# A guarded fallback recurrence moved to another branch, and two gather buffers kept side by side, in a one-core RWKV kernel with two mixtures of experts

## The chip, the cores and the metric

The kernel runs on one core of one Trainium2 chip. The metric is device time in microseconds of one execution. Before the change, three runs took 936.85, 937.87 and 938.58 us; the median is 937.87 us.

## What is computed

Three steps follow each other, each one feeding the next:

```python
# 1. recurrence over S = 768 steps, for B = 4 batches, H = 8 heads, D = 48
cur   = u * k[t] (x) v[t];  y[t] = r[t] . (state + cur)
state = w[t] * state + k[t] (x) v[t]
x = y as rows: N = 3072 tokens, 384 columns
# 2. first mixture, top 1 of E = 8 experts, F = 1024
out[mask] = gate_w * sigmoid(x @ w_output_gate)[e] * (relu(x @ w1[e]) @ w2[e])
# 3. second mixture, top 2 of 8, with noise on the logits
logits += log1p(exp(x @ w_noise)) * noise
out[mask] += top2_w * (relu(x @ w1[e]) @ w2[e])
```

The decays `w` of this input lie between 0.8 and 0.95. The fast form of step 1 is good for decays from 0.625 to 1.25 (`W_MIN`, `W_MAX`); for other decays the kernel holds a step-by-step recurrence that runs only where a flag says so.

## The kernel before, in words

**Step 1** works on 24 blocks of 128 steps (6 chunks times 4 batches), software-pipelined over several stages. Each block's rows go to the DRAM table `xrow`, the block is routed (`Route1`), and for each token an indirect DMA from GpSimd (`scatter`, L106, after a one-element `spacer` memset, L105) writes an entry into `tab1` at the token's place in its expert's list. ScalarE watches the decays (`guard`), and the largest excess becomes `flags[0]` (L373, `flag(wk, 0, ...)`).

**Work laid under step 1.** The first 224 tokens of expert 0 are known before the last blocks are routed. A generator, `early` (L793 to L827), takes them through both layers of expert 0; its steps are spread over the end of step 1 by `take(fill)`, and the rest of them, `take(fill, 99)`, closes it. It is TensorE work: three matmuls for each product (`mm3`, L175 to L177: high times high, low times high, high times low), 128x224 each, with ScalarE (`hh`, L813) and VectorE (`hl`, L814) splitting each hidden block.

**The first branch.** Ahead of that last piece stands `go = nc.values_load(flags[:, 0:1])` and `tc.If(go > 0)` with `recurrence(bank)` inside (L930 to L933). Every engine reads the flag and branches. The flag is 0 here, so the body is jumped over. In the built program the body holds 301 instructions on TensorE, 268 on VectorE, 149 on SyncE, 121 on GpSimd and 90 on ScalarE. After it come the last two scatters into `tab1`, `rank_experts` on VectorE (it sorts the experts by load; L378 to L386), and on SyncE the loads of the entry lists of experts 0, 1 and 2 (`load1`, L485) and of expert 1's weights (`w_load`, L147 and L150, into two `raw` buffers; ScalarE and VectorE split them into high and low parts, L162 and L163).

**First mixture.** For each expert `gather1` (L1097) fetches its rows from `xrow` by indirect DMA, four gathers of up to 118 rows. Expert 0 gathers into buffer `xg10`, expert 1 into `xg11`, expert 2 into `xg10` again. `xg10` stands in the pool `es` from the start. `xg11` is opened at L1086 in the pool `m1`, whose memory belonged to step 1 until then. `xprep1` (L1116 to L1118) turns the rows on TensorE, 3 times 4 transposes for an expert; they stand in steps 5, 6 and 7 of the expert before. `up1` and `down1` are the two layers, the second two steps behind the first. `left_over` (L397) sets `flags[1]` where tokens did not fit into the experts' windows.

**The second branch** (L1261, L1262) stands at the end of the first mixture, with `overflow(0)` inside: the tokens that did not fit. It is not taken either; its body holds 201 instructions on TensorE, 200 on VectorE, 162 on GpSimd, 146 on SyncE, 140 on ScalarE. A third one like it (L1379) ends the second mixture.

**Second mixture.** `gather2` (L1052), `xprep2` (L1069), `up2` and `down2` work the same way, 128 rows at a time. The last short block of an expert multiplies with a float32 copy of w2, which `whole` writes (L1297) into a buffer `w2f` of 2 x 1536 columns.

[...]

Of the kernel before, what the change touches and what calls it, by code (L numbers as in the profile page):

```python
# [9 lines left out]
F32 = mybir.dt.float32  # L10
# [10 lines left out]
N, DM, E, F = B * S, H * D, 8, 1024  # L21
# [23 lines left out]
JE = 2  # L45
# [19 lines left out]
def rwkv_moe_kernel(ctx, tc, r, k, v, w, rT, kT, wT, rkv, u, g1, a1, a2, g2, noise, b1, b2, out):  # L65
# [114 lines left out]
        w_slots(wp, i)  # L180
    es = ctx.enter_context(tc.tile_pool(name="es", bufs=1))
    nz0 = es.tile([128, J1, E], F32, name="nz0")
    xg1 = [es.tile([128, J1, XW], F32, name="xg10")]
    seen = [con.tile([128, 1], F32, name=f"seen{i}") for i in range(2)]


# [209 lines left out]

    def left_over(wk, m, early):  # L397

        n = wk.tile([1, E + 1], F32, name="n")
        w = windows(wk, m)  # L400
        nc.vector.tensor_tensor(n[:, 0:E], base[m][0:1], slot0[0:1], OP.subtract)
        nc.vector.tensor_tensor(n[:, 0:E], n[:, 0:E], w[0:1], OP.subtract)
        nc.vector.tensor_scalar(n[:, E:E + 1], seen[m][0:1], -1.0, float(early), OP.mult, OP.add)
        flag(wk, 1 + m, n, 0.0)


    def recurrence(bank):
        with ExitStack() as c2:
            fb = c2.enter_context(tc.tile_pool(name="fb", bufs=1))
            DQ = D // 4  # L410
            st = fb.tile([128, DQ, D], F32, name="st")
            nc.vector.memset(st, 0.0)
            sel = fb.tile([128, 32], F32, name="sel")
            nc.vector.tensor_copy(sel, ident[:, 0:32])
            for q in range(1, 4):
                nc.vector.tensor_tensor(sel, sel, ident[:, 32 * q:32 * q + 32], OP.add)
            uq = fb.tile([128, DQ], F32, name="uq")
            for q in range(4):
                nc.sync.dma_start(uq[32 * q:32 * q + 32], rows(u, q * DQ, [[0, B], [D, H], [1, DQ]]))

            def over_e(a):
                return a[:, :, None].to_broadcast([128, DQ, D])

            with tc.For_i(0, S // TS, 1) as blk:
                t = {}
                for nm, src in (("r", r), ("k", k), ("w", w), ("v", v)):
                    n = D if nm == "v" else DQ
                    t[nm] = fb.tile([128, TS, n], F32, name="f" + nm)
                    src = src.rearrange("b h s d -> (b h) s d")
                    for q in range(4):  # L430
                        d0 = 0 if nm == "v" else q * DQ
                        nc.sync.dma_start(t[nm][32 * q:32 * q + 32], src[:, bass.ds(blk * TS, TS), d0:d0 + n])
                yq = fb.tile([128, TS, D], F32, name="yq")
                for s in range(TS):
                    kv = fb.tile([128, DQ, D], F32, name="kv")
                    nc.vector.tensor_tensor(kv, over_e(t["k"][:, s, :]),
                                            t["v"][:, s:s + 1, :].to_broadcast([128, DQ, D]), OP.mult)
                    cur = fb.tile([128, DQ, D], F32, name="cur")
                    nc.vector.tensor_tensor(cur, kv, over_e(uq), OP.mult)
                    nc.vector.tensor_tensor(cur, cur, st, OP.add)  # L440
                    nc.vector.tensor_tensor(cur, cur, over_e(t["r"][:, s, :]), OP.mult)
                    nc.vector.tensor_reduce(yq[:, s, :], cur.rearrange("p d e -> p e d"), AX.X, OP.add)
                    nc.vector.tensor_tensor(st, st, over_e(t["w"][:, s, :]), OP.mult)
                    nc.vector.tensor_tensor(st, st, kv, OP.add)
                y = fb.tile([32, TS, D], F32, name="y")
                for h in range(2):
                    p = bank("kp")
                    half = slice(h * TS // 2, (h + 1) * TS // 2)
                    nc.tensor.matmul(p[0:32, 0:TS // 2 * D], sel, yq[:, half, :].rearrange("p a b -> p (a b)"),
                                     start=True, stop=True)  # L450
                    nc.vector.tensor_copy(y[:, half, :].rearrange("p a b -> p (a b)"), p[0:32, 0:TS // 2 * D])
                for b in range(B):
                    dst = xrow[bass.ds(blk * TS + b * S, TS), 0:DM].rearrange("t (h e) -> h t e", h=H)
                    nc.sync.dma_start(dst, y[b * H:(b + 1) * H])
            clear_table(tab1)
            nc.vector.tensor_copy(base[0], slot0)
            nc.vector.memset(seen[0], 0.0)
            nc.vector.memset(ent1[:, 0, 0:JE], 0)
            nc.vector.memset(ent1[:, 0, 0:JE, 0], N)
            for c in range(NC):  # L460
                L = bank("lp")[:, 0:B * 2 * E].rearrange("p (a b) -> p a b", a=B)
                for b in range(B):
                    x = fb.tile([C, DM], F32, name="x")
                    nc.sync.dma_start(x, xrow[b * S + c * C:b * S + (c + 1) * C, 0:DM])
                    p = bank("kp")[:, 0:DM].rearrange("p (a b) -> p a b", a=KD)
                    for j in range(KD):
                        nc.tensor.transpose(p[:, j, :], x[:, j * 128:(j + 1) * 128], ident)
                    xT = fb.tile([128, KD, C], F32, name="xT")
                    nc.scalar.copy(xT, p)
                    for j in range(KD):  # L470
                        nc.tensor.matmul(L[:, b, :], xT[:, j, :], g1s[:, j, :], start=(j == 0), stop=(j == KD - 1))
                g = Route1(fb, L, c * C)
                for _ in g.choose():
                    pass
                g.exps()
                g.rank(bank("kp"))
                for _ in g.place():
                    pass
                for b in range(B):
                    g.enter(b, "tab1 again")  # L480
# [12 lines left out]
    with ExitStack() as c2:  # L493
# [433 lines left out]
        RT[r2].rank(bank("kp"))  # L927
        take(RT[r2].place(), 9)
        take(fill, 2)
        go = nc.values_load(flags[:, 0:1], min_val=0, max_val=1)  # L930
        with tc.If(go > 0):  # L931
            recurrence(bank)
            nc.vector.memset(RT[r2].slot, E * NT)  # L933
        for j in range(RT[r2].nj):
            RT[r2].enter(j, "tab1")
        rank_experts(wk, 0)
# [8 lines left out]


    def overflow(m):
        w1, w2, tab, least, early = ((a1, a2, tab1, min(W1), WE), (b1, b2, tab2, min(W2), NA))[m]
        with ExitStack() as c2:
            fb = c2.enter_context(tc.tile_pool(name=f"ov{m}", bufs=1))  # L950
            bank = banks(psum, p="23", y="5")
# [130 lines left out]
    with ExitStack() as c2:  # L1082
        wk = c2.enter_context(tc.tile_pool(name="m1", bufs=2))
        bank = banks(psum, hp="01", tp="23", yp0="4", yp1="5", yp2="6", lp="7", up="01456")
        X, Q, HT, Y = {}, {}, {}, {}
        xg1.append(wk.tile([128, J1, XW], F32, name="xg11", bufs=1))  # L1086
        GATH, SCAT = [], []

        def part(e):
# [170 lines left out]

    go = nc.values_load(flags[:, 1:2], min_val=0, max_val=1)  # L1261
    with tc.If(go > 0):  # L1262
        overflow(0)


# [4 lines left out]
    with ExitStack() as c2:  # L1270
# [7 lines left out]
            xprep2(POOL[half], e, k, half, bank("tp"))  # L1278


        REST = dict(w=wk.tile([128, 2 * WH], F32, name="w2f"), h=wk.tile([128, NF, 64], F32, name="hf"))

        def quarters(q):
            return 4 if q <= 32 else 2 if q <= 64 else 1
# [151 lines left out]
```

## Time and profile before

| | us |
|---|---|
| median of three runs | 937.87 |
| the profiled execution | 937.88 |
| its span, first to last instruction | 936.2 |
| TensorE busy | 892.2 (95%) |
| VectorE busy | 516.2 (55%) |
| GpSimd busy | 402.7 (43%) |
| ScalarE busy | 395.3 (42%) |
| mean granted TensorE clock | 0.974 |

In the rows of this document PE is TensorE's matmul, PEld its weight load, DVE VectorE, ACT ScalarE, POOL GpSimd and SP SyncE; a name with q (PEldq, SPq) is that engine's instruction queue. `out<-in` are the program's names of the tiles. What stands in brackets at the end of a row is how long the engine was idle before it and what ended that. Tile `b` is a bank of PSUM, `xg` a gathered block of rows, `ent` an entry list, `tab` a table of entries.

### The profile page before, as it was taken

The numbers are of one execution on the slowest core, as the hardware profiler recorded it, in microseconds if no ns is written. First come the engines' busy times: TensorE is split into PE (matmuls) and PEld (weight loads), VectorE is DVE, ScalarE is ACT, GpSimd is POOL, SyncE is SP. The second block draws the span as 40 slices with busy tenths as digits, with TensorE's granted clock in tenths as the row PEclk, the third lists the DMA queues.
The fourth block names the chain that finished last, engine by engine and source line by source line (L and its number), as shares of the span: only waits on it lengthen the run. The fifth ranks groups of instructions, "written<-read, shape, count | busy, mean of one in ns | idle before, by whom it ended". The sixth has DMA issues, their size and how long they took to land. (4 is left out here: it accounts for less than half of the span.)

```text
span 936.2 us, 16625 instructions
## 1 busy us (share of the span) xinstructions
PE 892.2 (95%) x6244; PEld 797.3 (85%) x6244; DVE 516.2 (55%) x1146; ACT 395.3 (42%) x862; POOL 402.7 (43%) x562
## 2 busy tenths in 40 slices
PE   8999999979799999999898999999999999999996
PEld 4887777769788999999787989889898998989995
DVE  7999999754355565556561555272543627244220
ACT  4556555333345455555441443342433425344320
POOL 3234554334244885598564441423424133242212
PEclk9999998799899999999998999999999999999998
DMA  9777664014645767676514653435444444443203
GB/s 206 180 212 181 180 172 140 28 37 132 182 124 136 183 166 174 151 185 131 160 26 106 148 134 85 76 115 104 104 88 92 133 76 122 102 102 85 34 9 44
DMA packets 91099, 113.39 MB, mean 121 GB/s; under 512 B 26002, under 2 KB 68895, under 8 KB 91000
## 3 DMA queue, kind: packets, MB, share of 16 engines
q1 hardware_dynamic: 65848, 80.87, 30.9%
q0 software_dynamic: 25152, 31.27, 18.3%
q8 instruction: 53, 0.87, 0.4%
q14 instruction: 46, 0.38, 0.2%
HBM read 86.96 MB, written 25.78 MB: 120 GB/s over the span
## 5 line engine op out<-in xcount | busy, mean ns | idle before, releaser
L106 POOL DMA_INDIRECT out<-yo,ent x54 | 84.6, 1567 | 275.6 <-ACT yo L1327 232.8
L175 PE MATMUL b<-xhi,w1h 128*128 128x512 f32 (+8 forms) x384 | 133.0, 346 | 0.0
L177 PE MATMUL b<-xhi,w1l 128*128 128x512 f32 (+8 forms) x384 | 132.1, 344 | 0.0
L176 PE MATMUL b<-xlo,w1h 128*128 128x512 f32 (+8 forms) x384 | 132.1, 344 | 0.0
L1071 DVE TENSOR_TENSOR xlo<-b,xhi 128x512 fp32r<-128x512 f32 (+8 forms) x48 | 27.1, 570 | 155.4 <-ACT xhi L1070 142.4
L1327 ACT ACTIVATE yo<-b,ent 128x384 f32<-128x384 f32 (+1 forms) x48 | 27.9, 582 | 166.8 <-issue 128.1
L1314 PE MATMUL b<-w2h,hah 128*128 128x384 f32 x256 | 88.8, 347 | 0.4 <-PEq L1262 0.4
L106 POOL DMA_INDIRECT tab<-en,si x60 | 79.8, 1330 | 19.0 <-issue 13.9
L1316 PE MATMUL b<-w2h,hal 128*128 128x384 f32 x256 | 86.9, 339 | 0.0
L1315 PE MATMUL b<-w2l,hah 128*128 128x384 f32 x256 | 86.8, 339 | 0.0
L175 PEld LDWEIGHTS b<-xhi,w1h 128*128 128x128 f32 x384 | 72.3, 188 | 11.8 <-issue 3.1
L647 POOL TENSOR_SCALAR_AFFINE_SELECT at<-at 128x512 f32<-128x512 f32 x48 | 38.8, 833 | 98.3 <-ACT at L646 98.3
L175 PE MATMUL b<-xh,w1h 128*128 128x224 f32 (+7 forms) x216 | 76.3, 353 | 3.8 <-PEq L931 3.1
L176 PEld LDWEIGHTS b<-xlo,w1h 128*128 128x128 f32 x384 | 72.4, 188 | 8.8 <-DVE xlo L1071 0.2
L177 PEld LDWEIGHTS b<-xhi,w1l 128*128 128x128 f32 x384 | 72.3, 188 | 8.6
L175 PE MATMUL b<-hh,w2h 128*128 128x224 f32 (+7 forms) x216 | 74.7, 346 | 0.0
L176 PE MATMUL b<-xl,w1h 128*128 128x224 f32 (+7 forms) x216 | 73.5, 340 | 0.1
L177 PE MATMUL b<-xh,w1l 128*128 128x224 f32 (+7 forms) x216 | 73.4, 340 | 0.0
L163 DVE TENSOR_TENSOR w1l<-raw,w1h 128x512 fp32r<-128x512 f32 x92 | 61.7, 685 | 21.0 <-ACT w1h L162 20.4
L1080 DVE SCALAR_TENSOR_TENSOR hal<-b,hah 128x512 fp32r<-128x512 f32 x64 | 44.2, 691 | 52.4 <-ACT hah L1079 52.2
L176 PE MATMUL b<-hl,w2h 128*128 128x224 f32 (+7 forms) x216 | 72.7, 336 | 0.0
L177 PE MATMUL b<-hh,w2l 128*128 128x224 f32 (+7 forms) x216 | 72.5, 336 | 0.0
(221 smaller groups left out, 2153.7 us busy)
## 6 DMA issues: line engine op xcount, KB each, us to landing
raw<-in_a SPq DMA_DIRECT2D x32, 768.0 KB, 9.5
raw<-in_b SPq DMA_DIRECT2D x30, 768.0 KB, 4.5
decay<-in_wT SPq DMA_DIRECT2D x24, 224.0 KB, 3.4
kT<-in_kT SPq DMA_DIRECT2D x24, 224.0 KB, 5.9
rT<-in_rT SPq DMA_DIRECT2D x24, 224.0 KB, 4.3
v<-in_rkv SPq DMA_DIRECT2D x24, 192.0 KB, 4.4
xrow<-x SPq DMA_DIRECT2D x24, 192.0 KB, 3.3
out<-z SPq DMA_DIRECT2D x6, 768.0 KB
```

The lines of the kernel that those rows point to most:

```text
L106: st = nc.gpsimd.indirect_dma_start(out=table, out_offset=bass.IndirectOffsetOnAxis(ap=idx, axis=0), in_=src, in_offset=None, bounds_check ...
L163: eng.tensor_tensor(c, a, b.bitcast(F32), OP.subtract)
L175: nc.tensor.matmul(ps, st[0], mv[0], start=start, stop=False)
L176: nc.tensor.matmul(ps, st[0], mv[1], start=False, stop=False)
L177: nc.tensor.matmul(ps, st[1], mv[0], start=False, stop=stop)
L647: nc.gpsimd.affine_select(at[:, hh], at[:, hh], [[0, HP], [1, C]], OP.is_gt, 0.0, base=0, channel_multiplier=-1)
L1071: nc.vector.tensor_tensor(t["lo"][:, k], p[:, 0:n], t["hi"][:, k].bitcast(F32), OP.subtract)
L1080: nc.vector.scalar_tensor_tensor(l, p[:, 0:n], 0.0, h.bitcast(F32), OP.max, OP.subtract)
L1314: nc.tensor.matmul(parts[0], h[:, f, sl], wh, start=(f == 0), stop=False)
L1315: nc.tensor.matmul(parts[0], h[:, f, sl], wl, start=False, stop=False)
L1316: nc.tensor.matmul(parts[0], l[:, f, sl], wh, start=False, stop=(f == NF - 1))
L1327: nc.scalar.activation(o, y, AF.Copy, scale=wgt2[:q, e, j:j + 1])
```

## The change

The recurrence goes from the first branch into the second, under a branch of its own; `left_over` puts `flags[0]` beside the other counts, so that the second branch is taken where either flag is set. What the first mixture then wrote from wrong rows is cleared and done again in `overflow(0)`, which starts at slot 0 (`least` is 0). Both gather buffers of the first mixture become halves of one tile `xgs` in `es`, open from the start to the end of the kernel; the float32 copy of w2 lies in that tile.

```diff
@@ pools
-    xg1 = [es.tile([128, J1, XW], F32, name="xg10")]
+    xgs = es.tile([128, 2 * J1 * XW], F32, name="xg1")
+    xg1 = [xgs[:, i * J1 * XW:(i + 1) * J1 * XW].rearrange("p (a b) -> p a b", a=J1) for i in range(2)]
@@ left_over
-        n = wk.tile([1, E + 1], F32, name="n")
+        n = wk.tile([1, E + 2], F32, name="n")
+        if m == 0:
+            nc.vector.tensor_copy(n[:, E + 1:E + 2], flags[:, 0:1])
+        else:
+            nc.vector.memset(n[:, E + 1:E + 2], 0.0)
@@ recurrence (its end)
             clear_table(tab1)
-            nc.vector.tensor_copy(base[0], slot0)
-            nc.vector.memset(seen[0], 0.0)
-            nc.vector.memset(ent1[:, 0, 0:JE], 0)
-            nc.vector.memset(ent1[:, 0, 0:JE, 0], N)
+            clear_table(tab2)
+            for t in base:
+                nc.vector.tensor_copy(t, slot0)
+            nc.vector.memset(seen[0], float(WE))
...
@@ the end of step 1
         take(fill, 2)
-        go = nc.values_load(flags[:, 0:1], min_val=0, max_val=1)
-        with tc.If(go > 0):
-            recurrence(bank)
-            nc.vector.memset(RT[r2].slot, E * NT)
         for j in range(RT[r2].nj):
             RT[r2].enter(j, "tab1")
@@ overflow
-        w1, w2, tab, least, early = ((a1, a2, tab1, min(W1), WE), (b1, b2, tab2, min(W2), NA))[m]
+        w1, w2, tab, least, early = ((a1, a2, tab1, 0, WE), (b1, b2, tab2, min(W2), NA))[m]
@@ first mixture
-        xg1.append(wk.tile([128, J1, XW], F32, name="xg11", bufs=1))
@@ the second branch
     go = nc.values_load(flags[:, 1:2], min_val=0, max_val=1)
     with tc.If(go > 0):
+        again = nc.values_load(flags[:, 0:1], min_val=0, max_val=1)
+        with tc.If(again > 0):
+            recurrence(banks(psum, kp="2", lp="7"))
         overflow(0)
@@ second mixture
-        REST = dict(w=wk.tile([128, 2 * WH], F32, name="w2f"), h=wk.tile([128, NF, 64], F32, name="hf"))
+        REST = dict(w=xgs[:, 0:2 * WH], h=wk.tile([128, NF, 64], F32, name="hf"))
```

In the built program of the change the second branch's body holds 515 instructions on TensorE, 488 on VectorE, 318 on SyncE, 301 on GpSimd and 242 on ScalarE. Outside the bodies each engine keeps the order of its work: the reads of the first flag and the first branch go, VectorE gets one instruction more in each `left_over`, and what wrote and read `w2f` names `xg`.

**GpSimd from the first branch to expert 1's gathers.** Before, from the end of the jump (semaphores in brackets are waited for; DMASW are those of GpSimd's DMAs, DMAHW those of SyncE's; `xg_107` is xg10, `xg_4008` is xg11; the 112-row gathers are expert 0's, the 118-row ones expert 1's):

```order
L931 ISA [waits Pool_49,DMASW4_49,DMASW5_49,DMASW3_49,DMASW6_49,DMASW2_49,DMASW7_49,DMASW1_49,DMASW0_49]
L931 UNCONDITIONAL_BRANCH
L105 MEMSET spacer 1x1 [waits Pool_49]
L106 DMA tab_66<-ent,slot 25600x2 [waits DMASW7_49,DMAHW7_49,DMASW0_49,DVE_49]
L105 MEMSET spacer 1x1 [waits Pool_49]
L106 DMA tab_66<-ent,slot 25600x2 [waits DMASW1_49]
L1097 DMA xg_107<-xrow,ent_81 112x392 [waits DMAHW4_49,DMAHW5_49,DMAHW3_49,DMAHW6_49,DMAHW0_49,DMASW2_49]
L1097 DMA xg_107<-xrow,ent_81 112x392 [waits DMASW3_49]
L1097 DMA xg_4008<-xrow,ent_81 118x392 [waits DMAHW2_49,DMAHW1_49,DMAHW3_49,DMASW6_49,DMAHW4_49,DMASW5_49,DMAHW5_49,DMASW4_49,DMAHW6_49,DVE_49,DMAHW7_49,PE_49,Activation_49]
L1097 DMA xg_4008<-xrow,ent_81 118x392 x3
```

And now (L1102 is the line of the gathers, L1119 that of the copy of the noise columns):

```order
L300 IOTA ent 128x2 [waits DMASW5_49,DMASW4_49]
L105 MEMSET spacer 1x1 [waits Pool_49]
L106 DMA tab_66<-ent,slot 25600x2 [waits DVE_49,Pool_49]
L105 MEMSET spacer 1x1 [waits Pool_49]
L106 DMA tab_66<-ent,slot 25600x2
L1102 DMA xg_107<-xrow,ent_81 112x392 [waits DMAHW6_49,DMAHW5_49,DMAHW7_49,DMAHW4_49,DMAHW3_49]
L1102 DMA xg_107<-xrow,ent_81 112x392
L1102 DMA xg_107<-xrow,ent_81 118x392 [waits DMAHW0_49]
L1102 DMA xg_107<-xrow,ent_81 118x392
L1102 DMA xg_107<-xrow,ent_81 118x392 [waits DMASW6_49]
L1102 DMA xg_107<-xrow,ent_81 118x392 [waits DMASW7_49]
L1119 COPY nz_106<-xg_107 112x16 [waits DMASW3_49,DMASW2_49]
```

The jump with its waits on all of GpSimd's own DMAs is gone, and expert 1's first gather waits for its entry list alone, not for VectorE, TensorE and ScalarE to be done with the memory of step 1.

**TensorE at the first branch.** Before (the rows of L424 stand in the body that is jumped over):

```order
L175 MATMUL b_2924<-hh,w2h_97 128x224
L176 MATMUL b_2924<-hl,w2h_97 128x224
L177 MATMUL b_2924<-hh,w2l_98 128x224
L930 TENSOR_LOAD flags [waits DVE_49]
L931 COMPARE_AND_BRANCH
L424 COMPARE_AND_BRANCH
```

And now:

```order
L175 MATMUL b_2924<-hh,w2h_97 128x224
L176 MATMUL b_2924<-hl,w2h_97 128x224
L177 MATMUL b_2924<-hh,w2l_98 128x224
L175 MATMUL b_2980<-xh,w1h_95 128x224 [waits DVE_49]
L176 MATMUL b_2980<-xl,w1h_95 128x224
L177 MATMUL b_2980<-xh,w1l_96 128x224
```

The matmuls of the next step of `early` follow directly.

**TensorE at the second branch.** Now (L429 is the first line of the recurrence that branches; before, the reading of the flag and one branch, L1261 and L1262, stood in the same place):

```order
L175 MATMUL b_6509<-xhi_6124,w1h_3126 128x512
L176 MATMUL b_6509<-xlo_6125,w1h_3126 128x512
L177 MATMUL b_6509<-xhi_6124,w1l_3127 128x512
L1266 TENSOR_LOAD flags [waits DVE_49]
L1267 COMPARE_AND_BRANCH
L1268 TENSOR_LOAD flags
L1269 COMPARE_AND_BRANCH
L429 COMPARE_AND_BRANCH
```

The second pair, L1268 and L1269, stands inside the first body and is jumped over with it.

## Rows read from the trace of the kernel before

**Rows 1.** The profile's page, busy time of each engine.

```profile
PE 892.2 (95%) x6244; PEld 797.3 (85%) x6244; DVE 516.2 (55%) x1146; ACT 395.3 (42%) x862; POOL 402.7 (43%) x562
```

**Rows 2.** Stretches: width, busy PE, PEld, DVE, ACT, POOL (count), granted clock, DMA share, GB/s.

```profile
200.00:222.00 22.00, 18.25 (x148) 17.79 (x146) 7.31 (x36) 3.92 (x14) 6.33 (x10) 0.92 0.31 93
222.00:250.00 28.00, 21.68 (x148) 20.55 (x149) 14.20 (x32) 11.79 (x28) 12.70 (x12) 0.82 0.55 134
...
400.00:450.00 50.00, 50.00 (x312) 47.65 (x311) 30.48 (x83) 25.83 (x56) 43.82 (x55) 1.00 0.63 146
```

**Rows 3.** One line's instructions, L931, the first branch: queue, count, ns, starts.

```profile
L931 POOLq EVENT_SEMAPHORE  x5: 17/43/43, 203.3 to 206.9; - x5
...
L931 PEldq COMPARE_BRANCH  x1: 4501/4501/4501, 203.0 to 203.0; - x1
```

**Rows 4.** TensorE in order of time, around the first branch: start, us.

```profile
207.71 0.40 PE L175 MATMUL b<-xh,w1h 128*128 128x224 f32 x1 [3.14 <-PEq L931]
...
211.30 0.28 PE L177 MATMUL b<-hh,w2l 128*128 128x224 f32 x1
...
212.42 0.27 PE L175 MATMUL b<-hh,w2h 128*128 128x224 f32 x1
```

**Rows 5.** GpSimd in order of time, from the first branch to expert 1's gathers.

```profile
207.75 0.09 POOL L105 MEMSET spacer<- 1x1 f32 x1 [4.44 <-DMA tab<-ent,slot]
...
215.55 0.97 POOL L1097 DMA_INDIRECT xg<-xrow,ent  x1 [4.31 <-issue]
...
223.93 1.65 POOL L1097 DMA_INDIRECT xg<-xrow,ent  x1 [6.17 <-ACT xh L1117]
...
229.79 2.15 POOL L1097 DMA_INDIRECT xg<-xrow,ent  x1 [0.30 <-issue]
```

**Rows 6.** TensorE in order of time, expert 1's first transposes and what follows.

```profile
234.66 0.26 PE L1116 MATMUL b<-ident,xg 118*128 118x118 f32 x1
235.11 0.32 PE L1116 MATMUL b<-ident,xg 118*128 118x118 f32 x1 [0.18 <-DMA xg<-xrow,ent]
239.76 0.46 PE L1116 MATMUL b<-ident,xg 118*128 118x118 f32 x1 [4.33 <-DMA xg<-xrow,ent]
241.19 0.46 PE L1116 MATMUL b<-ident,xg 118*128 118x118 f32 x1 [0.97 <-DMA xg<-xrow,ent]
241.32 0.54 PE L175 MATMUL b<-hh,w2h 128*128 128x224 f32 x1
...
245.28 0.63 PE L1116 MATMUL b<-ident,xg 118*128 118x118 f32 x4
```

**Rows 7.** Stretches 208 to 211 and 222 to 228, columns as in group 2.

```profile
208.00:211.00 3.00, 3.00 (x16) 3.00 (x16) 1.78 (x8) 0.36 (x1) 1.83 (x3) 0.50 0.04 9
...
222.00:228.00 6.00, 5.16 (x29) 4.77 (x30) 3.85 (x13) 3.27 (x10) 3.46 (x3) 0.74 0.06 8
```

**Rows 8.** Expert 1's weights: SyncE's issue and ScalarE's first split in order of time.

```profile
228.82 0.39 SPq L147 DMA_DIRECT2D raw<-in_a  x1
```

**Rows 9.** ScalarE in order of time, the first split of that load.

```profile
238.31 0.62 ACT L162 CAST w1h<-raw 128x512 fp32r<-128x512 f32 x1 [5.10 <-DMA raw<-in_a]
```

**Rows 10.** Tile raw from 190 to 300 us, its loads.

```profile
DMA to landing us min/median/max: 7.3/8.4/9.5
```

**Rows 11.** One line's instructions, L1262, the second branch.

```profile
L1262 PEldq EVENT_SEMAPHORE  x2: 51/51/51, 493.6 to 493.8; - x2
...
L1262 PEldq COMPARE_BRANCH  x1: 362/362/362, 489.7 to 489.7; - x1
...
L1262 DVEq COMPARE_BRANCH  x1: 63/63/63, 494.7 to 494.7; - x1
```

**Rows 12.** TensorE's first wait for gathered rows after the second branch.

```profile
504.39 0.75 PE L1069 MATMUL b<-ident,xg 128*128 128x128 f32 x2 [1.72 <-DMA xg<-xrow,ent]
```

**Rows 13.** GpSimd's first gather after the second branch, in order of time.

```profile
500.11 1.00 POOL L1052 DMA_INDIRECT xg<-xrow,ent  x1 [5.52 <-DMA ent<-tab]
```

**Rows 14.** VectorE in order of time, one element in left_over.

```profile
222.42 0.13 DVE L403 TENSOR_SCALAR n<-seen 1x1 f32<-1x1 f32 x1
```

More of the change, by code (lines that the diff above doesn't have):

```diff
@@ L404, in left_over, with recurrence @@
         flag(wk, 1 + m, n, 0.0)
-    def recurrence(bank):
+    def recurrence(bank, r=r, k=k, v=v, w=w, u=u):
         with ExitStack() as c2:
@@ L455, in recurrence @@
             clear_table(tab1)
-            nc.vector.tensor_copy(base[0], slot0)
-            nc.vector.memset(seen[0], 0.0)
-            nc.vector.memset(ent1[:, 0, 0:JE], 0)
-            nc.vector.memset(ent1[:, 0, 0:JE, 0], N)
+            clear_table(tab2)
+            for t in base:
+                nc.vector.tensor_copy(t, slot0)
+            nc.vector.memset(seen[0], float(WE))
+            nc.vector.memset(seen[1], 0.0)
+            nc.vector.memset(place_of[0], 0.0)
+            nc.vector.memset(ent2[:, 0, 0:CUT], 0)
+            nc.vector.memset(ent2[:, 0, 0:CUT, 0], N)
             for c in range(NC):
```

## The prediction, made before the change was run

> **What bounds the kernel now.** I read the page first: TensorE is busy for 892.2 of 936.2 us, no other engine for more than 516.2 [rows 1]. So the time can only fall where TensorE stands still or runs slowly. The view by stretches says where. In the stretch from 400 to 450 us, in the first mixture, TensorE has work all the time at full clock. Between 200 and 250 us it has not: it is busy for 18.25 of 22 us and then for 21.68 of 28, at a granted clock of 0.92 and 0.82 [rows 2]. In these 50 us stand both things that the change touches, so I read TensorE, GpSimd and the queues there in order of time.
>
> Two holes are to be seen. At the first branch TensorE's queue spends 4.501 us in the jump [rows 3], and the array waits 3.14 us, from 204.57 to 207.71 [rows 4]. GpSimd waits 4.44 us there, for its own scatters to land [rows 5]. The second hole is at expert 1's first transposes. TensorE waits 0.18, 4.33 and 0.97 us for gathered rows [rows 6], because GpSimd began expert 1's gathers only at 223.93, 6.17 us after it was free [rows 5]. The name beside that wait, ScalarE's `xh`, is only what came last; by the order in the section on the change the gather waited for three engines to leave step 1's memory, where `xg11` was opened.
>
> After each hole comes a slow stretch. [...] After the second hole eighteen matmuls take from 241.32 to 245.28, 0.220 each [rows 6].
>
> **The change, part by part.**
>
> *The first branch goes.* TensorE gets back the wait of 3.14 us. It then had no hole, and I take it that the slow stretch behind it goes too: 3.59 us for seventeen steps against 17 x 0.112 = 1.90, so 1.69. Bounds for this term: 0 and 1.69; I take 1.69, since the same matmuls ran at 0.112 just behind. Together 4.83. The chain beside it gains as much: GpSimd's last two scatters no longer stand behind 207.75, where its wait of 4.44 us ended [rows 5]. Entry lists, expert 0's gathers (from 215.55 [rows 5]) and expert 1's first weight loads follow these scatters; with 4.4 to 4.8 us they stay where they were against TensorE. `rank_experts`, seven short VectorE instructions, now runs between two steps of `early`; TensorE's second layer runs two steps behind the first and covers it.
>
> *Expert 1's gathers wait for their list alone.* They follow expert 0's two, of 0.97 us and 0.3 of issue each: 215.55 - 4.8 + 2 x 1.27 = 213.3. From the first to the fourth it was 5.86 us, and the fourth took 2.15 [rows 5], so GpSimd starts the fourth near 219.2. TensorE comes to these transposes at 234.66 - 4.83 = 229.8 [rows 6]. The fourth gather landed by 241.19, 11.4 us after its start at 229.79, beside two weight loads. As slow as that again, it would land at 219.2 + 11.4 = 230.6 and cost 0.8; if it lands in 10.6 or less it costs nothing. So 0.18 + 4.33 + 0.97 = 5.48 us go, and with them the slow stretch: 3.96 - 18 x 0.112 = 1.94. Bounds here: 6.6 and 7.4. I take 7.42, for the loads that it runs beside start 4 us and more before the gathers and not, as then, in their midst.
>
> *What is late next.* Expert 1's second half of w1 is loaded into a buffer that its first half must leave, so its issue at 228.82 [rows 8] moves with TensorE, to 224.0, and no further. Before, ScalarE got it at 238.31 after a wait of 5.10 [rows 9], 9.5 us after the issue; that was hidden behind the wait for the gathers. Without them TensorE would go through the last three steps of expert 0 in some 6.5 us from 229.8. ScalarE stands at that load with the next hidden block behind it. At 9.5 us the data come at 233.5, and TensorE waits about 1.3 us for that block and 0.7 for the last transposed columns behind the fourth load. At 7.3 us, the shortest of these loads [rows 10], it waits for nothing. I take 1.0, for the median of 8.4, between 0 and 2.0.
>
> *The second branch jumps further.* TensorE jumped 301 instructions in 4.501 us [rows 3] and 201 in 0.362 [rows 11]; now it is 515 there, so I take the long price. Its queue reached this branch at 489.7, but its array had work until 493.6 [rows 11]. A jump until 494.2 makes it 0.6 late, and that falls into its wait of 1.72 for the next gather [rows 12]. That gather, GpSimd's at 500.11 [rows 13], waits for its list and for every engine to have passed the branch. VectorE is the last to come, at 494.7 [rows 11]; with 4.5 us it is through at 499.2, so 0.9 us are left. Cost: 0. Bounds: 0 and, if nothing hid it, 4.501 - 0.362 = 4.1. [...]
>
> *Edits at no cost.* One element more in each `left_over` is one VectorE instruction of about 0.13 us [rows 14], on an engine that then waits for ScalarE. `xgs` instead of `w2f`: the same instructions on the same data, long after the last gather into it. The recurrence's and the overflow's new lines are not run.
>
> *Sum.* 3.14 + 1.69 + 5.48 + 1.94 - 1.0 = 11.25 us. The profiled execution took 937.88 us, 0.01 above the median of the three runs, so the forecast is 937.88 - 11.25 = **926.6 us**. I let it reach the end because TensorE is full in the first mixture behind expert 1's start, as in the stretch from 400, and GpSimd's part there, though it is busy for 43.82 of 50 us [rows 2], starts from what TensorE gives it.
>
> **The rivals.**
>
> *The transfers take the wait's place.* Expert 1's gathers now run beside its first two weight loads, and expert 2's beside the next two. If they hold each other up as the load of 9.5 us was held up [rows 9], TensorE stands at the same place as before and only the branch is won: 937.88 - 4.83 = 933.0. For it speaks that ScalarE waited for that load until 238.31, just ahead of 239.76 [rows 6]; against it that expert 1's gathers start 10.6 us earlier, 213.3 and not 223.93, and so share the transfers' engines with other loads over a longer stretch.
>
> *The second branch takes it back.* Place: L1267, on the engine that leaves it last, which GpSimd's gather at 500.11 [rows 13] waits for. Price: each microsecond that the longest jump takes over 5.4 (500.11 - 494.7) is one microsecond at the end. Twice 4.501 would give 926.6 + 3.6 = 930.2. It decides when the jump lasts over 5.4 + 11.25 = 16.7 us: then the kernel is slower than 937.9. Nothing in the trace jumps for longer than 4.501.
>
> *The gain is lost on the way.* If GpSimd's chain of scatters, not TensorE, sets when the second mixture can start, arriving 11 us early at it means waiting 11 us longer: 937.9. Its 43.82 of 50 us [rows 2] speak for it; against it, that TensorE does not wait at all in that stretch.
>
> **How the numbers follow.** Forecast 0.80, range of its own 924 to 928.5. Transfers 0.10 (933.0). Second branch, part given back, 0.04 (930.2), all of it and more 0.03 (over 939.8 if the jump lasts over 18.6 us). Lost on the way 0.03 (937.9). The range for all takes in: no new wait, 925.6; in addition the slow stretch that I left in, between 222 and 228 us, where the clock was 0.74 [rows 7], that is 3.1 us at half speed, worth 1.6 if it goes: 924.0; a microsecond for the spread of runs (936.85 to 938.58): 923.0. Upwards the transfers' case and half a microsecond, 933.5. A measurement of this kernel can tell 0.2%, 1.9 us, from no change: faster 0.80 + 0.10 + 0.04 = 0.94, the same 0.03, slower 0.03.
>
> **What would show it.** Right: no matmul idle near 204.6 and none at half clock until 211; the 118-row gathers' first start near 213; no wait of L1121 (the transposes' new line) for `xg` over 1 us; TensorE's transposes of expert 1 from about 229.8 on; a long jump at L1267 on TensorE and VectorE with GpSimd's next gather not later against the last scatter than before. Wrong in size: a wait of ScalarE for `raw` that ends after 234 and a TensorE hole behind it. Wrong altogether: the second mixture starting at the same time as before, or a jump at L1267 that ends after GpSimd's list has landed.

## The result, and the profile after

The changed kernel took 925.76 us, the median of four runs (924.22 to 928.43), against 938.23 for the kernel before in the same runs: a ratio of 0.9871, 95% interval 0.9837 to 0.9905. The profiled execution spans 925.3 us and the one before 936.2, so 10.9 us have to be found.

The page, and the stretches of [rows 1, 2], of the changed kernel:

```profile
PE 889.2 (96%) x6244; PEld 795.3 (86%) x6244; DVE 515.4 (56%) x1148; ACT 395.5 (43%) x862; POOL 402.6 (44%) x562
```

```profile
200.00:222.00 22.00, 19.90 (x155) 19.11 (x154) 7.83 (x38) 4.79 (x16) 12.22 (x15) 0.89 0.39 110
222.00:250.00 28.00, 28.00 (x201) 25.75 (x201) 16.00 (x29) 15.53 (x35) 5.17 (x7) 0.98 0.67 203
...
198.00:204.00 6.00, 6.00 (x42) 5.93 (x43) 4.17 (x28) 1.45 (x6) 2.34 (x6) 0.72 0.03 3
...
220.00:224.00 4.00, 4.00 (x24) 4.00 (x24) 1.75 (x4) 1.99 (x5) 0.72 (x2) 0.61 0.35 93
```

From 222 to 250 TensorE is busy for all 28 us, where it was for 21.68. Two slow stretches are left, 198 to 204 (clock 0.72) and 220 to 224 (0.61).

TensorE in order of time, the places of [rows 4, 6] and then the second branch and the gathers behind it:

```profile
205.91 0.27 PE L177 MATMUL b<-hh,w2l 128*128 128x224 f32 x1
...
217.22 0.29 PE L1121 MATMUL b<-ident,xg 112*128 112x112 f32 x1 [0.99 <-DMA xg<-xrow,ent]
218.39 0.70 PE L1121 MATMUL b<-ident,xg 112*128 112x112 f32 x5 [0.88 <-DMA xg<-xrow,ent]
...
230.34 0.57 PE L1121 MATMUL b<-ident,xg 118*128 118x118 f32 x4
...
232.76 0.57 PE L1121 MATMUL b<-ident,xg 118*128 118x118 f32 x4
...
485.94 0.65 PE L1322 MATMUL b<-w2h,hah 128*128 128x384 f32 x1 [4.55 <-DVEq L1267]
...
497.39 0.27 PE L1075 MATMUL b<-ident,xg 58*128 58x58 f32 x1 [0.99 <-DMA xg<-xrow,ent]
```

The matmul that began at 211.30 [rows 4] now begins at 205.91, 5.39 earlier: the hole at the first branch is gone. The transposes of 245.28 [rows 6] now begin at 232.76, 12.52 earlier: the wait for expert 1's rows is gone too. New are two waits for expert 0's rows (0.99, 0.88) and a hole of 4.55 us behind the second branch. Matmuls are matched in this way below: by order, one trace against the other; what the lead grows over a stretch is what that stretch gained.

GpSimd, the places of [rows 5, 13]:

```profile
210.51 0.96 POOL L1102 DMA_INDIRECT xg<-xrow,ent  x1 [4.35 <-DMA ent<-tab]
...
213.03 1.65 POOL L1102 DMA_INDIRECT xg<-xrow,ent  x1 [0.30 <-issue]
...
218.87 1.64 POOL L1102 DMA_INDIRECT xg<-xrow,ent  x1 [0.30 <-issue]
...
481.09 1.30 POOL L106 DMA_INDIRECT tab<-en,si  x1 [0.22 <-issue]
...
490.48 1.00 POOL L1058 DMA_INDIRECT xg<-xrow,ent  x1 [8.08 <-DMA ent<-tab]
```

Expert 1's gathers follow expert 0's at once, and not 6.17 us later [rows 5].

ScalarE's split of the load of [rows 9], and the second branch's line, as in [rows 11]:

```profile
230.29 0.62 ACT L162 CAST w1h<-raw 128x512 fp32r<-128x512 f32 x1 [1.40 <-DMA raw<-in_a]
```

```profile
L1267 POOLq EVENT_SEMAPHORE  x6: 17/30/1521, 483.4 to 485.4; - x6
...
L1267 DVEq EVENT_SEMAPHORE  x2: 21/21/21, 485.8 to 485.9; - x2
...
L1267 PEldq COMPARE_BRANCH  x1: 3657/3657/3657, 477.6 to 477.6; - x1
...
L1267 DVEq COMPARE_BRANCH  x1: 72/72/72, 482.7 to 482.7; - x1
```

TensorE's queue has its 3.66 us while the array still has work, until 481.4. VectorE comes to the branch at 482.7 and is through 3.1 us later, and TensorE's next matmul waits until then.

### The profile page after: what moved, and what is told of

The parts are those of the page before. It is cut to its first block, busy times and chain, and to the rows that moved or that the text cites. A ratio compares the mean times of both kernels' runs of the same rounds, so it can differ in the third digit from the quotient of the medians.

```text
span 925.3 us, 16594 instructions
## 1 busy us (share of the span) xinstructions
PE 889.2 (96%) x6244; PEld 795.3 (86%) x6244; DVE 515.4 (56%) x1148; ACT 395.5 (43%) x862; POOL 402.6 (44%) x562
## 4 chain that ended last, share of the span: by engine, by line
PE 71%; DVE 8%; DMA 7%; issue 7%; POOL 3%; ACT 3%; SPq 0%; POOLq 0%; DVEq 0%; ACTq 0%
PE b L175 14%; PE b L176 13%; PE b L177 13%; PE b L1322 6%; PE b L1324 6%; PE b L1323 6%; PE b L1075 2%; PE b L719 2%; DMA xg<-xrow,ent 2%; DVE cp L634 1%; DMA tab<-en,si 1%; PE b L652 1%; PE b L1318 1%; POOL out L106 1%; DVE g L622 1%
## 6 DMA issues: line engine op xcount, KB each, us to landing
decay<-in_wT SPq DMA_DIRECT2D x24, 224.0 KB, 3.9
kT<-in_kT SPq DMA_DIRECT2D x24, 224.0 KB, 4.7
rT<-in_rT SPq DMA_DIRECT2D x24, 224.0 KB, 5.9
```

## The experiments

Where the 10.9 us lie is read from this table: for each kernel, what a stretch gained against the trace of the kernel before (us; the stretches are in that trace's time; negative is lost).

| stretch | after | again (e10) | again (e8) | e1 | e2 | e3 | e4 | e5 | e6 | e7 | e9 | e11 | e12 |
|---|---|---|---|---|---|---|---|---|---|---|---|---|---|
| 199.9 to 213.5, first branch | 3.84 | 3.84 | 3.84 | 0.28 | 3.82 | 3.31 | 4.61 | 3.83 | 3.27 | 4.98 | 3.83 | 3.83 | 3.83 |
| 213.5 to 232, expert 0's rows | -1.08 | -1.18 | 1.48 | -0.47 | -0.73 | -0.07 | -1.54 | -1.30 | -2.95 | 1.49 | -1.17 | -1.35 | -0.89 |
| 232 to 248, expert 1's rows | 8.26 | 8.25 | 8.15 | 8.26 | 0.70 | 8.25 | 0.99 | 8.25 | 8.25 | 3.86 | 8.24 | 8.25 | 8.25 |
| 476 to 515, second branch | -0.50 | 0.56 | -0.13 | -1.06 | 0.68 | 0.07 | 0.47 | -1.88 | 2.81 | 0.19 | 2.69 | -1.33 | 0.14 |

For the changed kernel the rest is 1.55 up to 199.9, -0.40 from 248 to 476 and -0.72 from 515 on; no edit touches the first and the last of these. Where e1 to e8, e11 and e12 ran, the kernel before itself took longer (952.69 us beside e1 to e4, 949.05 beside e5 to e8, 960.99 beside e11 and e12; 938.82 beside e9 and e10), and the traces there have further holes between 248 and 476 that the first two traces, e9 and e10 don't have; so these kernels are read by stretch, and by ratio only roughly.

**Each half of the change alone.** e1 is the kernel before with

```diff
-    xg1 = [es.tile([128, J1, XW], F32, name="xg10")]
+    xgs = es.tile([128, 2 * J1 * XW], F32, name="xg1")
+    xg1 = [xgs[...] for i in range(2)]
-        xg1.append(wk.tile([128, J1, XW], F32, name="xg11", bufs=1))
-        REST = dict(w=wk.tile([128, 2 * WH], F32, name="w2f"), ...)
+        REST = dict(w=xgs[:, 0:2 * WH], ...)
```

> The kernel before with both gather buffers standing through and w2's float32 copy in them; the first branch keeps the recurrence. Two causes (my theory): the wait of TensorE for expert 1's rows goes (5.48 us and the slow stretch behind it, 1.94), the hole of 3.1 us at the first branch stays: 937.9 - 7.4 = 930.5 us, up to 931.5 if ScalarE's wait for expert 1's second load costs 1. Rival A, the branch alone was worth it and the transfers keep expert 1's rows late: 936 to 938, with the wait at expert 1's first transposes still over 3 us.

e2 is the changed kernel with these lines back as they were.

> The changed kernel with the second gather buffer and the float32 copy back where they were; only the recurrence is moved. My theory: no hole near 204, the wait at expert 1's first transposes stays, 5 us earlier: 937.9 - 4.8 = 933.1 us, and 1 less gained if the longer second jump costs something. Rival A: 926. Rival B, the longer jump takes back what the shorter first gave: 936 to 938. If the two parts add up, the gains of this kernel and of the one with the buffers alone sum to the 11 to 12 us of the change.

Measured: e1 0.9936 of the time before (0.9891 to 0.9981), e2 0.9962 (0.9924 to 1.0001). In order of time, e1 and then e2, TensorE and GpSimd:

```profile
206.62 0.34 PE L175 MATMUL b<-xh,w1h 128*128 128x224 f32 x1 [2.86 <-PEq L932]
...
234.03 0.57 PE L1116 MATMUL b<-ident,xg 118*128 118x118 f32 x4
```

```profile
232.52 0.32 PE L1121 MATMUL b<-ident,xg 118*128 118x118 f32 x1 [2.74 <-DMA xg<-xrow,ent]
...
235.04 0.46 PE L1121 MATMUL b<-ident,xg 118*128 118x118 f32 x1 [2.20 <-DMA xg<-xrow,ent]
```

```profile
218.01 1.65 POOL L1102 DMA_INDIRECT xg<-xrow,ent  x1 [6.22 <-PE b L1121]
```

With the buffers alone the hole at the branch stays and the wait for expert 1's rows goes; with the branch alone it is the other way round, and GpSimd again waits some 6 us for engines to leave step 1's memory. Over the first three stretches e1 gains 8.07 and e2 3.79; together 11.86, the change 11.02. The two causes add up, so rival A falls: each half gains at its own place and nothing at the other's. Rival B falls too, since e2's last stretch lost nothing.

**The longer second jump.** e3 leaves the recurrence for other decays out:

```diff
-        again = nc.values_load(flags[:, 0:1], min_val=0, max_val=1)
-        with tc.If(again > 0):
-            recurrence(banks(psum, kp="2", lp="7"))
         overflow(0)
```

> The changed kernel without the recurrence for other decays at all (its way for such inputs is left out; the rest is unchanged), so the second branch jumps 201 instructions on TensorE and 200 on VectorE as before. Theory C: the hole of 4.55 us at L1322 behind the second branch is VectorE's jump, and it goes, but the list of gathered rows is late next, so 0.5 to 1.5 us are gained: 924.3 to 925.3 us. Rival D: the hole and the slow stretch behind it stand on the path and all of 4.55 + 1.7 comes back: 919.5. Rival E, which I forecast: 0, 925.8.

Measured: 0.9837 (0.9795 to 0.9879); the interval would hold theory D too, so the stretch decides. TensorE in order of time, and the branch's line:

```profile
498.21 0.41 PE L1319 MATMUL b<-w2h,hah 128*128 128x384 f32 x1 [0.52 <-PEq L1267]
507.78 0.59 PE L1075 MATMUL b<-ident,xg 128*128 128x128 f32 x2 [0.88 <-DMA xg<-xrow,ent]
510.58 0.36 PE L1075 MATMUL b<-ident,xg 58*128 58x58 f32 x1 [2.21 <-DMA xg<-xrow,ent]
```

```profile
L1267 DVEq EVENT_SEMAPHORE  x2: 21/21/21, 499.6 to 499.7; - x2
...
L1267 PEldq COMPARE_BRANCH  x1: 3654/3654/3654, 493.9 to 493.9; - x1
...
L1267 DVEq COMPARE_BRANCH  x1: 72/72/72, 499.0 to 499.0; - x1
```

VectorE passes in 0.6 us and the hole is 0.52, but TensorE then waits 0.88 and 2.21 for gathered rows. The stretch gives 0.07, amid the 0.56, -0.13 and -0.50 of the kernel with the recurrence in it: rival D falls. Theory C is right about the hole, which is VectorE's passage; of its gain nothing is to be seen, as rival E forecasts, though among executions that differ by 1.06 us a gain of 0.5 would not be seen either. TensorE's own queue took its 3.65 us here too, so the hole of 4.55 was not its own jump.

**The length of the first jump.** e4 is the kernel before with the recurrence's loop over chunks cut to a quarter:

```diff
-            for c in range(NC):
+            for c in range(NC // 4):
```

> The kernel before with the recurrence under its first branch cut to a quarter of its chunks (its way for other decays is left incomplete; TensorE has 76 instructions to jump and not 301, VectorE 173 and not 268). My theory, the hole is the jump's length and GpSimd's wait is a second matter: TensorE has no hole at the first branch and its jump takes under 0.5 us; GpSimd still waits some 4.4 us there, so expert 0's gathers stay near 215.5 and TensorE waits 3 to 5 us for them; expert 1's gathers come 4 to 5 us earlier and TensorE waits under 1.5 us for those: 932 to 934 us. Rival F, the hole is the flag's reading or GpSimd's wait and not the jump: the hole stays at 3 us, 937.9.

Measured: 0.9941 (0.9905 to 0.9976). The first branch's line, then the second branch's (L1262), and TensorE in order of time:

```profile
L931 POOLq EVENT_SEMAPHORE  x3: 17/17/43, 202.3 to 202.5; - x3
...
L931 PEldq COMPARE_BRANCH  x1: 358/358/358, 202.0 to 202.0; - x1
...
L1262 PEldq COMPARE_BRANCH  x1: 3530/3530/3530, 496.5 to 496.5; - x1
...
L1262 DVEq EVENT_SEMAPHORE  x2: 21/21/21, 504.7 to 504.8; - x2
```

```profile
218.21 1.12 PE L1116 MATMUL b<-ident,xg 112*128 112x112 f32 x6 [2.19 <-DMA xg<-xrow,ent]
...
232.26 0.32 PE L1116 MATMUL b<-ident,xg 118*128 118x118 f32 x1 [1.30 <-DMA xg<-xrow,ent]
235.60 0.46 PE L1116 MATMUL b<-ident,xg 118*128 118x118 f32 x1 [3.01 <-DMA xg<-xrow,ent]
```

The jump took 0.358 us instead of 4.501 [rows 3] and the hole is gone: it was the body that is jumped over, not the flag's reading, so rival F falls. The time is the one expected (0.9941 of 937.9 is 932.4), but by another sum: TensorE waits 2.19 us for expert 0's rows and not 3 to 5, and 4.31 for expert 1's and not under 1.5. GpSimd did not wait 4.4 us: it was through its semaphores at 202.5, not 206.9 [rows 3], so its wait too belonged to the body. Expert 1's gathers kept their wait, as in e2.

e4 shows one thing more. It leaves the second branch as it was, 201 instructions on TensorE and 200 on VectorE, and only shortens the code ahead of it; yet TensorE's queue takes 3.530 us there and not 0.362 [rows 11], and VectorE, which comes at 501.5, 3.2 us and not 0.6. So the number of instructions jumped over does not set the price.

**The hole behind the second branch.** e5 puts two of the eight blocks of `ahead` behind the branch:

```diff
-        for f in range(3, NF):
+        for f in range(3, 6):
             ahead(f)
...
         overflow(0)
+    for f in range(6, NF):
+        ahead(f)
```

> The changed kernel with the last two of the eight hidden blocks that are computed ahead (18 matmuls of 0.233 us) put behind the second branch instead of ahead of it, so that TensorE has 4.2 us of work while VectorE jumps. Theory G: the hole of 4.55 us at L1322 goes, but the chain from GpSimd's last scatter to the gathered rows is as long as before and is late next; TensorE waits 3 to 5 us more for xg behind it and the time stays within 1 us of the changed kernel's. Rival D: the hole stood on the path, 4 to 6 us are gained.

Measured: 0.9910 (0.9875 to 0.9946), beside 0.9899 for the changed kernel in the same runs. TensorE in order of time:

```profile
495.60 0.47 PE L175 MATMUL b<-xhi,w1h 128*128 128x512 f32 x1 [0.41 <-PEq L1267]
511.59 0.47 PE L1075 MATMUL b<-ident,xg 128*128 128x128 f32 x2 [3.12 <-DMA xg<-xrow,ent]
514.55 0.35 PE L1075 MATMUL b<-ident,xg 58*128 58x58 f32 x1 [2.49 <-DMA xg<-xrow,ent]
```

Theory G in kind: the hole is 0.41 and the waits for rows are 5.61 together; rival D falls again. In size it was worse than expected, 1.4 to 2.4 us less in the stretch than the three executions of the changed kernel.

e6 has, besides, the last expert's slots earlier:

```diff
         for k in range(KD):
+            if k == 1 and between:
+                between()
...
-        ahead(2)
-        routing_b(e)
+        ahead(2, lambda: routing_b(e))
+        route2_c(Q[e], T1[e][0], "tab2")
         rank_experts(wk, 1)
         w_split(1, 0, W2B, 2)
-        route2_c(Q[e], T1[e][0], "tab2")
```

> As the kernel with two blocks behind the branch, and the last expert's ranks and slots (routing_b) are computed in the middle of the third block ahead, not behind it, with rank_experts and one split of weights behind the scatters' issue, so GpSimd's six last scatters start 1.5 to 2 us earlier against TensorE. Theory G: the chain of scatters, list and gathers sets the end here, so 1.5 to 2.5 us are gained on the changed kernel. Rival: if TensorE's work or VectorE's jump sets it, nothing is gained.

Measured: 0.9885 (0.9824 to 0.9946), and 2.81 in the stretch, in a profiled execution that was the longest of the four (947.75 us; the others 933.16 to 945.05). So the reading rests on e9, the same kernel again in more executions, beside the changed kernel.

> The kernel with the ranks and slots earlier and two blocks behind the branch, again with more rounds: by the stretch from the second branch on it gained some 3 us on the changed kernel, so a ratio to the kernel before that is 0.003 lower than the changed kernel's in these same runs. Rival: its gain there was chance like the waits at L1121, and the two ratios agree.

> The changed kernel beside it: 0.985 to 0.990 of the time before, hole of 4.5 us at L1322, a gain of 3.8 us at the first branch and of 9 us at expert 1's rows against the trace of the kernel before.

Measured: 922.96 us for e9, 0.9824 (0.9794 to 0.9854); 924.60 for e10, 0.9842 (0.9815 to 0.9869). In e9, GpSimd's first of the six scatters and TensorE:

```profile
475.79 1.30 POOL L106 DMA_INDIRECT tab<-en,si  x1 [1.31 <-DVE s L360]
```

```profile
483.14 0.47 PE L175 MATMUL b<-xhi,w1h 128*128 128x512 f32 x1 [1.40 <-DVE hal L1088]
498.74 0.27 PE L1075 MATMUL b<-ident,xg 58*128 58x58 f32 x1 [2.48 <-DMA xg<-xrow,ent]
```

GpSimd's wait for VectorE there is 1.31 instead of 3.09 us, and the stretch gains 2.69, 2.13 more than in e10. It comes twice, in e6 and e9. The times are 0.0018 apart and not the 0.003 expected; their intervals overlap, so e9 beats the kernel before for certain and the changed kernel by its trace only.

**Which wait the hole was.** Why should TensorE, with hidden blocks to multiply, wait for VectorE to pass? Its first matmul behind the branch writes PSUM bank 7, and the recurrence, now in the body, has its logits there. e11 moves them:

```diff
-            recurrence(banks(psum, kp="2", lp="7"))
+            recurrence(banks(psum, kp="2", lp="3"))
```

> The changed kernel with the recurrence's logits in PSUM bank 3 instead of bank 7, and nothing else. Theory K: TensorE's hole of 4.55 us behind the second branch is no jump of its own and no data that it needs; its first matmul there writes bank 7, which VectorE reads inside the body that is jumped over, so it waits until VectorE has passed the branch. With bank 3 the hole falls to 0.5 us. The list of gathered rows is late next, so TensorE waits 3 to 4 us for xg instead of 1 and the stretch from 476 to 515 changes by less than 1 us: 0.984 to 0.988 of the time before. Rival: VectorE's last hidden block is what the matmul waits for; then the hole stays at 4.5.

e12 adds the earlier slots of e6, with all eight blocks ahead of the branch.

> Bank 3 as beside it, and the last expert's ranks and slots in the middle of the third block ahead as in the kernel that did best, but all eight blocks ahead of the branch as in the changed kernel. If the list sets the end of this place and the hole is only bank 7, the stretch gains 2 to 3 us on the changed kernel as with two blocks behind the branch: 0.981 to 0.985 of the time before. Rival: the two blocks behind the branch were what gained; then the stretch stays within 1 us of the changed kernel's.

Measured: e11 0.9893 (0.9834 to 0.9951), e12 0.9862 (0.9801 to 0.9923). The branch's line and TensorE of e11:

```profile
L1267 PEldq COMPARE_BRANCH  x1: 3417/3417/3417, 503.5 to 503.5; - x1
...
L1267 DVEq COMPARE_BRANCH  x1: 72/72/72, 508.5 to 508.5; - x1
```

```profile
507.68 0.42 PE L1322 MATMUL b<-w2h,hah 128*128 128x384 f32 x1 [0.45 <-PEq L1267]
...
519.50 0.82 PE L1075 MATMUL b<-ident,xg 128*128 128x128 f32 x2 [3.00 <-DMA xg<-xrow,ent]
522.26 0.35 PE L1075 MATMUL b<-ident,xg 58*128 58x58 f32 x1 [1.94 <-DMA xg<-xrow,ent]
```

Theory K: with another bank TensorE goes on at 507.68, before VectorE has even come to the branch (508.5), and the hole is 0.45. e4 shows the same from the other side: its second body has no recurrence in it and does not name bank 7, VectorE is through only at 504.8, and TensorE goes on at 500.86 after 0.45 us. In e11 the waits for rows take the hole's place, 4.94 us, and the stretch ends at -1.33; the hole was hidden time to a microsecond. e12's stretch is 0.14: there its rival stands, the earlier slots alone gain nothing. In e12 SyncE issued the list at 504.75 and the gather began 4.59 us later, where e9 has 3.11 (488.30 to 491.41). The profile names a matmul as what the gather waited for; the queue's own rows tell more, GpSimd's at the gather's line and VectorE's behind the branch:

```profile
L1058 POOLq EVENT_SEMAPHORE  x12: 17/43/2802, 504.8 to 508.5; - x12
```

```profile
L1268 DVEq EVENT_SEMAPHORE  x2: 21/21/21, 507.8 to 507.9; - x2
```

The wait of 2.80 us ends at 507.98, 0.04 after VectorE's last signal behind the branch, and it is that signal's semaphore that it waits for. So the gather needs its list and VectorE's passage. In e12 the list is early and VectorE late, since all its hidden blocks come ahead of the branch; in e9, with two of them behind it, VectorE is through at 486.8, ahead of the list's issue; in e5 VectorE is through at 499.7 and the list is issued only at 504.57. So e5, e11 and e12 gain nothing, and e6 and e9, with the slots earlier and the blocks behind, gain 2.7 to 2.8: it takes both.

**Expert 0's rows.** e7 issues expert 1's first two weight loads on GpSimd's queue behind expert 0's gathers; e8 is the changed kernel again.

```diff
-        w_load(0, 1, W1A)
-        w_load(0, 1, W2A)
...
         gather1(0)
+        for w in (W1A, W2A):
+            w_load(0, 1, w, nc.gpsimd)
         gather1(1)
```

> The changed kernel with expert 1's first two weight loads issued on GpSimd's queue behind expert 0's gathers instead of on SyncE's ahead of them. Theory H: TensorE's two waits at L1121 for expert 0's rows (0.99 and 0.88 us) come from sharing the transfers with these loads; they fall under 0.5 together and 1 to 1.9 us are gained, if expert 1's gathers, 2 to 3 us later, still land in time (by 230). Rival: the waits stay, since the gathers are short of nothing that the loads take, and the time is 0 to 2 us longer.

> The changed kernel again, on the chip of these runs, to compare with: 0.985 to 0.99 of the time before; the hole at L1322 of 4.5 us, two waits at L1121 of 0.5 to 1 us and no wait at expert 1's transposes over 1 us, if these were not chance.

Measured: e7 0.9925 (0.9887 to 0.9963), e8 0.9899 (0.9860 to 0.9939). TensorE of e7, then of e8:

```profile
230.15 0.32 PE L1119 MATMUL b<-ident,xg 118*128 118x118 f32 x1 [2.36 <-DMA xg<-xrow,ent]
```

```profile
215.86 1.07 PE L1121 MATMUL b<-ident,xg 112*128 112x112 f32 x6 [0.68 <-ACT yt L836]
...
273.23 0.73 PE L175 MATMUL b<-xh,w1h 128*128 128x440 f32 x1 [4.66 <-issue]
```

In e7 no wait for expert 0's rows is left, but e8 has none either, with the loads where they were, so TensorE's waits do not decide it. The landings do. By the last signal of each gather in the trace, expert 0's two landed 2.9 and 3.0 us after their starts in e7, and 6.6 and 6.6 in the changed kernel's first trace, 7.5 and 6.8 in e10; in e8 TensorE turned the second one's rows 5.8 us after its start. So theory H holds for the transfers, in one execution of e7: beside the two loads they land some 3 to 4.5 us later. Whether TensorE then waits is a matter of a microsecond, and that differs between executions. What e7 costs is plain: expert 1's gathers come too late, a wait of 2.36 us, 4.4 us lost in the stretch. That the waits of 0.99 and 0.88 were chance, as the expectation for e8 allowed, is half true: e10 has them again (1.98 together). The changed kernel has both outcomes, 1.48 and -1.1, with no edit between them. Some 1.5 of the 2.6 us between them is the clock, by an estimate from two stretches: in e8 it stayed at 1.00 there (below), where in the first trace it was 0.61 for 4 us (220 to 224, above).

```profile
216.00:224.00 8.00, 7.67 (x63) 7.05 (x63) 5.97 (x17) 5.26 (x13) 3.12 (x3) 1.00 0.38 90
```

In e3 it fell there too (0.54 from 221 to 223), with no wait for these rows. So the fall does not need that wait, and its cause is open.

## Why the prediction was right

The prediction was 926.6 us with 11.25 us gained; it came out 925.76, 12.5 below the median of the kernel before in the same runs; in the profiled executions the stretches sum to 10.95, as the spans do (10.9). The mechanism was right at both places. Of the sizes, three were off and cancelled, which is luck: the four places gave 10.52 together, and 0.43 came from stretches that I had no term for.

- *The first branch, 4.83.* It gave 3.84. By the starts of the matmuls the hole gave 3.3 and the slow stretch behind it 1.7, as forecast, but 1.2 was lost ahead of them, from 199.9 on. The forecast's 1.69 rests on starts in the trace before: seventeen matmuls from 207.71 to 211.30 and ten from there to 212.42 [rows 4], 0.211 and 0.112 us each, with the clock at 0.50 from 208 to 211 [rows 7]. The step that failed is "It then had no hole, and I take it that the slow stretch behind it goes too". In the trace before, the stretch from 198 to 204 ran at full clock; in the changed kernel it runs at 0.72 (above), so the slow stretch moved ahead of where the hole had been. In e4 and e7, without a hole as well, the clock stayed at 1.00 (e4 below), and this place gave 4.61 and 4.98, near to the 4.83; so the slow stretch does not always come, and what decides it is open.

The same stretch of the kernel before:

```profile
198.00:204.00 6.00, 4.94 (x51) 4.51 (x51) 5.15 (x35) 2.04 (x9) 2.27 (x4) 1.00 0.09 9
```

The same stretch of e4:

```profile
198.00:204.00 6.00, 5.25 (x49) 4.88 (x47) 4.69 (x31) 1.82 (x7) 2.36 (x5) 1.00 0.07 7
```

- *Expert 1's gathers, 7.42.* They gave 8.26, and within 0.11 of that in every kernel that has both buffers and issues nothing ahead of these gathers. Their first and fourth starts were forecast at 213.3 and 219.2 and came at 213.03 and 218.87; TensorE's transposes were forecast for 229.8 and came at 230.34. Of the 8.26, 5.48 are the waits of [rows 6] and 1.9 the slow stretch behind them, both as forecast. The other 0.84 lies at a term that I had left out, the four transposes between the waits: from the first of them to the matmul at 241.32 it was 6.66 us [rows 6], 1.18 more than the waits, and now it is 0.34.
- *What is late next, -1.0.* The load was issued at 225.13 (forecast 224.0), ScalarE waited until 230.29, and TensorE did not wait for it at all. The loss came from a step that I had put at nothing: that expert 0's gathers "stay where they were against TensorE". They came 5.04 us earlier, TensorE 5.39, and they landed 6.6 us after their starts, the first of them 0.4 later than before; so TensorE waited 0.99 and 0.88, where it had waited 0.68 for ScalarE. They land so late beside the two weight loads (2.9 and 3.0 us in e7, where these come behind them), which stood ahead of them before the change too; that leaves them within a microsecond of TensorE, and I had looked at their starts alone. The stretch lost 1.08, by chance what I had taken off for the other cause; in e8 it gained 1.48.
- *The second branch, 0.* It gave -0.50, 0.56 and -0.13 in three executions, and e3 and e5 show that this is cover and not a cheap jump. But the place was wrong: I had TensorE 0.6 late by its own jump. It was 4.55 late, waiting for VectorE to pass, on account of bank 7 (e11), and VectorE reaches the branch only when its last hidden block is done. I had read in the trace when each engine passes, and not which of them TensorE's next matmul would have to wait for. The hole and the slow clock behind it (0.50 from 486 to 488) took 5.7 us of TensorE's lead. The cover was the 1.72 for the next gather [rows 12], a second wait of 1.94 at 507.07 and the slow clock behind that one (0.50 from 506 to 510); of these only 0.99 is left. The sign that I gave, GpSimd's gather not later against the last scatter, was not met: 500.11 - 493.29 = 6.82 before, 490.48 - 481.09 = 9.39 after (7.65 in e10, 6.07 in e3). One part of it shows in the trace: GpSimd now waits 1.52 us in its passage (above) and is done with it at 486.24, and SyncE issues the list at 486.26, 5.17 after the last scatter's start; it was 4.36.
- *The price of a jump by its length* was the weak premise: 201 instructions took TensorE 0.362 us before [rows 11], 3.654 in e3 and 3.530 in e4, which did not touch that branch. Length does not set it: now 515 took 3.657 (3.66 above), where 301 had taken 4.501 [rows 3], and in e4 only the code ahead of the branch was shorter. What sets it, no run here shows. The long price that I took for 515 was an estimate from two rows.
- *The rivals.* Transfers in the wait's place: no wait at expert 1's rows in the kernels with both buffers, except in e7, which delayed the gathers. The second branch taking it back, and the gain lost on the way: the lead of 12.52 us at 232.76 was still 12.2 at the end of the first mixture and 11.7 behind the second branch.

## What to carry to other kernels

A tile whose memory came from a pool of the stage before made its first writer wait for every engine that used that memory, 6.17 us [rows 5], though the profile named only the last; with a buffer that stands through, that gather began 0.30 us after the one ahead of it (213.03), and its place gained 8.26. A branch that is not taken can still couple the engines through what its body names: here TensorE's next matmul into bank 7 waited 4.55 us until VectorE had passed, and 0.45 with another bank (e11), and GpSimd's next gather waited 2.80 us (e12). But removing such a hole gave nothing while a chain beside it was as long (e5 -1.88 and e11 -1.33 in the stretch); look for that chain first. Do not count a slow clock behind a hole as won with the hole: here one of two went and one came back ahead of its place (0.72 from 198 to 204).

## What was not expected of the hardware

- The slow stretch at the first branch: from 198 to 204 TensorE ran at a clock of 1.00 in the kernel before, where a hole followed at 204.57, and at 0.72 in the changed kernel, where none did (in e4 and e7 it was 1.00 without a hole).
- TensorE's passage of a branch with 201 instructions in its body: 0.362 us before, 3.530 in e4 and 3.654 in e3. In e4 only the code ahead of the branch had changed, and VectorE's passage went from 0.6 to 3.2 us with it.
- GpSimd's time for an indirect DMA differed between numbers of rows, and not upwards: expert 0's gathers of 112 rows took 0.96 and 0.94 us, expert 1's of 118 rows 1.65 (GpSimd's rows above), and of the scatters into `tab2` those of 124 rows took 1.30 and those of 128 rows 0.97 to 1.05. What sets it stays open; no run here changed the number of rows.
- In e1 to e8, e11 and e12 TensorE stood still for 2.5 to 10 us at one to three places between 270 and 400 us, put down to nothing that the profile names, as at 273.23 in e8 above, or to ScalarE, which waited for nothing that it names. What it was stays open.
